# Router scores of a second token block on VectorE, and the last attention chunks two steps later

## The chip, the cores and the metric

The kernel runs on one core of one Trainium2 chip. The metric is device time in microseconds: the median of three runs of the kernel before is 455.16 us (454.08 to 455.33). One execution was profiled: 457.24 us, with a span of 455.1 us from the first instruction to the last.

The engines are TensorE (PE; its weight loads are PEld), VectorE (DVE), ScalarE (ACT), GpSimd (POOL) and SyncE (SP), which here only issues DMAs.

## The reference

Three layers follow each other. Decayed linear attention over 2 batches, 8 heads, 768 positions of 64 dimensions; a feed-forward layer; and a mixture of experts with one expert a token and a skip score:

```
x   = attention(q, k, v, lam)          # (1536, 512) after the heads are joined
h   = x @ w_in                          # 512 -> 2048
g   = where(h > 0, h, exp(min(h, 0)) - 1)
x2  = g @ w_out                         # 2048 -> 512
do  = (x2 @ w_skip) > 0
logits = x2[do] @ w_gate                # 8 experts
e   = argmax(logits); gate = softmax(logits)[e]
out = x2;  out[do] += gate * (relu(x2 @ w1[e]) @ w2[e])
```

The router's scores (8 logits and the skip score) decide comparisons, so they are computed in float32. The large matmuls split each operand into a high part and a residue and multiply in three passes.

## The kernel before

The 1536 tokens are four blocks of 384 (block 0 to 3), each of three chunks of 128 tokens: chunk 0 to 11. Chunks 6 to 8 make block 2, chunks 9 to 11 block 3.

The feed-forward layer runs in 64 units, each one slice of 128 of the 2048 hidden columns for one block. A unit is `ff1_mm` (12 matmuls into a PSUM bank named h, L496), `ff1_act` on ScalarE, the max on VectorE (L516), the high part on ScalarE (L522), the residue on VectorE (`ff1_lo`, L527) and `ff2` (three groups of three matmuls, L543). The units 0 to 31 mix blocks 0 and 1; units 32 to 47 are block 2, 48 to 63 block 3.

From unit 24 on, a loop walks the units. Its step n issues the max and high part of unit n+1, `ff1_mm` of unit n+2, the residue of unit n+1 and `ff2` of unit n. So TensorE alternates one `ff1_mm` and one `ff2`, and VectorE works one unit ahead. There is no scheduler in this stretch: each engine runs in the order in which the code is written. Other work is hung into the steps with five tables, keyed by the step: Y and A after `ff1_mm` (and ahead of the residue), C behind the residue, B behind the second `ff2` group and `ff1_act`, Z behind the third `ff2` group. The helper `put(table, step, function, arguments)` fills them. J is 24, NF 16, N 64, CPB 3, CPS 6.

What is hung in:
- `put_chunks(n, c0)`: attention of three chunks, at steps n, n+2, n+4, n+5. `at_X` issues on TensorE the outputs of the chunk before (L292, 64x64 matmuls) and the key-value products and scores of the next (L364, L330), which share an h bank with `ff1_mm`; then the masks on VectorE (L338). `at_X2` evacuates the chunk before (L427, L431), starts the two state updates (L382, four instructions each) and the query scaling on GpSimd (L345). `at_kdec2` is the key scaling on GpSimd (L350). Before, one state update stands in `at_X2` behind the evacuation and the other in table Z. The sets start at steps 24 and 37.
- `put_routes(n, c0)`: the routing of a block. `route_T` transposes a chunk on TensorE (L583) and copies it to SBUF; `route_logits` is four matmuls by the gate (L598); `route_pick` (L632 to L642), `route_exp`, `route_slot` and `route_send` are small VectorE instructions, with an exponential on ScalarE and an indirect DMA from GpSimd (L700) that scatters the chunk's rows to its experts; `route_rank` is two small matmuls (L655, L658). Block 0 starts at step 37, block 1 at 32, block 2 at 48.
- `route_dots`: for block 0 the scores are not matmuls. VectorE multiplies the chunk by a broadcast gate row and sums in the same instruction (L620, with a second small instruction that reads the accumulator): 9 rows times 3 chunks, 27 products in steps 28 to 37. The gate rows lie in one buffer of the ring `big` (two buffers of 128 x 2048 floats): three rows in turn, the fourth quarter takes the product itself, which nobody reads.
- `conv_piece`: from step 49, the split of one piece of the experts' weights (L138 on ScalarE, L139 on VectorE); `load_pieces` loads two of them into a buffer of `big`.

Of the kernel before, what the change touches and what calls it, by code (L numbers as in the profile page):

```python
# [8 lines left out]
F32 = mybir.dt.float32  # L9
# [4 lines left out]
ALU = mybir.AluOpType  # L14
# [14 lines left out]
LEAD = 21  # L29
TAIL1 = 8  # L30
E = 8
EF = 1024
# [28 lines left out]
def kernel(  # L61
# [49 lines left out]
    places = const.tile([P, P], F32, name="places")  # L111
    rk = const.tile([P, 1], F32, name="rk")
    cnt = const.tile([P, E], F32, name="cnt")
    nx = const.tile([P, E + 1], F32, name="nx")
    nxi = const.tile([P, E + 1], I32, name="nxi")
# [5 lines left out]
    lp = mid.tile([P, 4, P], F32, name="lp")  # L121
    kd = mid.tile([P, H, 1], F32, name="kd")
    state = mid.tile([P, 4, P], F32, name="state")
# [271 lines left out]
    def at_out(c, banks):  # L395
# [7 lines left out]
        for m in range(2):  # L403
            for b, r in ((0, 0), (1, 1), (1, 0), (0, 1)):
                inter(c, r, m, 1 - r, b)

    def at_out2(c):

        nc.tensor.drain()
        for m in range(2):  # L410
            for b, r in ((0, 0), (1, 1), (1, 0), (0, 1)):
                inter(c, r, m, r, b)
# [188 lines left out]

    dots = [(e, c) for e in range(E + 1) for c in range(CPB)]
    dotted, cols = [0], []

    def open_cols():
        t = big(F32).rearrange("p (s d) -> p s d", s=4)
        cols.extend(t[:, i] for i in range(4))
        for e in range(3):
            load_col(e)

    def load_col(e):
        nc.sync.dma_start(out=cols[e % 3], in_=wgt[e:e + 1, :].broadcast_to([P, DM]))

    def route_dots(k):
        for _ in range(k):
            e, c = dots[dotted[0]]
            dotted[0] += 1
            if e == 0:
                lg_t[c] = sm([P, E + 1], F32, "lg", CPB)
            nc.vector.tensor_tensor_reduce(  # L620
                out=cols[3], in0=x2_t[c][:, 0:DM], in1=cols[e % 3], scale=1.0, scalar=0.0,
                op0=ALU.mult, op1=ALU.add, accum_out=lg_t[c][:, e:e + 1])
            if c == CPB - 1 and e + 3 <= E:
                load_col(e + 3)

# [91 lines left out]
    if True:  # L717
# [169 lines left out]

        def at_X2(c, nxt):
            if c is not None:
                at_evac_hi(c)  # L890
                at_evac_lo(c)
                if c == CPS + 1:
                    open_cols()
                elif c == CPS + 2:
                    load_chunk(c + 1)
                elif c + 2 < NCH:
                    load_chunk(c + 2)
            if nxt is not None:
                at_state2(nxt, 0)
                at_qd2(nxt)  # L900
# [4 lines left out]
        def put_routes(n, c0):  # L905
            for i in range(CPB):
                if c0:
                    put(B, n + i, route_T, c0 + i)
# [6 lines left out]
        def put_chunks(n, c0):  # L915
            for c, nxt, m in ((None, c0, n), (c0, c0 + 1, n + 2), (c0 + 1, c0 + 2, n + 4),
# [11 lines left out]
        left = len(dots)  # L928
# [366 lines left out]
```

## Time and profile before

| | |
|---|---|
| median of three runs | 455.16 us (454.08 to 455.33) |
| profiled execution | 457.24 us |
| its span | 455.1 us |
| TensorE busy | 438.2 us, 96% |
| VectorE busy | 314.3 us, 69% |
| ScalarE busy | 241.0 us, 53% |
| GpSimd busy | 78.9 us, 17% |

A step is read from TensorE's timeline: from the first L496 row of one `ff1_mm` to that of the next. Step 24 starts at 143.77 us, step 32 at 185.84, step 37 at 211.22, step 44 at 252.54, step 48 at 269.35. Matmuls are pipelined and their ends are modelled, so a row's length is no measure of a group's cost; the distance from start to start is.

### The profile page before, as it was taken

The page shows a single profiled execution, that of the slowest core. Times are in us where ns is not written, and L with a number is a line of the kernel's source. Part 1 is how long each engine was busy: PE and PEld are TensorE (multiplying, and loading weights), DVE is VectorE, ACT ScalarE, POOL GpSimd, SP SyncE. Part 2 cuts the span into 40 slices and gives each one's busy share as a digit, 9 for nine tenths or more (in the row PEclk, how much of TensorE's full clock was granted, in tenths as well). Part 3 has the DMA queues.
Part 4 walks back from the last instruction along what each step waited for, and adds up shares of the span by engine and source line. Part 5 has one row for each costly group of instructions (what it writes and reads, how often), then busy time and mean ns, then how long its engine had stood idle before and what let it go on. Part 6 is the DMA issues. An engine that isn't in the chain of part 4 may idle for free.

```text
span 455.1 us, 8009 instructions
## 1 busy us (share of the span) xinstructions
PE 438.2 (96%) x3123; PEld 379.5 (83%) x3123; DVE 314.3 (69%) x647; ACT 241.0 (53%) x402; POOL 78.9 (17%) x100
## 2 busy tenths in 40 slices
PE   8889999999999999999999999999999999999993
PEld 7778898879898888988778899889988788888882
DVE  4889999999532448687675225765545789999970
ACT  3456776666444333433232444466642788888840
POOL 4532002201200021014143000220004202222111
PEclk9989999999999999999999999999998999999998
DMA  8999602796001034310320024353446789999300
GB/s 303 401 423 420 238 19 92 232 127 200 0 2 71 5 127 167 125 47 34 108 101 15 0 95 160 118 196 116 149 148 270 256 313 394 371 373 366 144 17 34
DMA packets 27406, 77.07 MB, mean 169 GB/s; under 512 B 4162, under 2 KB 9290, under 8 KB 25312
## 3 DMA queue, kind: packets, MB, share of 16 engines
q1 hardware_dynamic: 25328, 71.35, 44.7%
q0 software_dynamic: 1600, 3.03, 1.8%
q10 hardware_dynamic: 432, 2.10, 1.2%
q8 instruction: 26, 0.43, 0.4%
q14 instruction: 20, 0.16, 0.1%
HBM read 68.18 MB, written 10.51 MB: 173 GB/s over the span
## 4 chain that ended last, share of the span: by engine, by line
PE 66%; DVE 16%; issue 7%; ACT 4%; DMA 4%; POOL 1%; SPq 1%; POOLq 0%; ACTq 0%; DVEq 0%
PE h L496 21%; PE y L543 16%; PE h L1075 8%; PE y L1100 6%; PE aux L543 5%; DVE v L176 3%; DVE v L179 3%; DMA big<-in_wff_dram 2%; ACT v L161 2%; DVE g L527 2%; DVE wa L190 2%; PE aux L598 1%; DVE v L173 1%; PE aux L292 1%; PE aux L1086 1%
## 5 line engine op out<-in xcount | busy, mean ns | idle before, releaser
L496 PE MATMUL h<-xT,wa 128*128 128x384 f32 x480 | 90.8, 340 | 0.6 <-DVE state L382 0.5
L496 PEld LDWEIGHTS h<-xT,wa 128*128 128x128 f32 x480 | 83.9, 188 | 4.3 <-issue 1.1
L543 PE MATMUL y<-wa,g 128*128 128x512 f32 x270 | 70.9, 402 | 1.1 <-DVE g L527 0.9
L522 ACT ACTIVATE g<-e 128x384 fp32r<-128x384 f32 x64 | 33.4, 522 | 48.6 <-DVE e L516 48.6
L543 PEld LDWEIGHTS y<-wa,g 128*128 128x128 f32 x270 | 49.0, 188 | 12.0 <-DVE g L527 1.8
L501 ACT ACTIVATE e<-h 128x384 f32<-128x384 f32 x64 | 31.1, 486 | 51.0 <-PE h L496 50.8
L516 DVE SCALAR_TENSOR_TENSOR e<-e,h 128x384 f32<-128x384 f32 x64 | 35.2, 549 | 32.3 <-ACT e L504 32.3
L496 PE MATMUL h<-xT,wb 128*128 128x384 f32 x288 | 54.7, 339 | 0.9 <-DVE lp L382 0.9
L496 PEld LDWEIGHTS h<-xT,wb 128*128 128x128 f32 x288 | 50.6, 188 | 3.6 <-issue 1.0
L527 DVE TENSOR_TENSOR g<-e,g 128x384 fp32r<-128x384 f32 x64 | 37.6, 588 | 16.0 <-ACT g L522 15.9
L543 PE MATMUL y<-wb,g 128*128 128x512 f32 x162 | 41.0, 397 | 0.2 <-DVE g L527 0.2
L700 POOL DMA_INDIRECT xe<-x,idx x12 | 12.1, 1009 | 141.8 <-DVE s L673 50.3
L1075 PE MATMUL h<-wa,xgT 128*128 128x512 f32 x144 | 36.5, 399 | 0.1
L543 PEld LDWEIGHTS y<-wb,g 128*128 128x128 f32 x162 | 30.0, 188 | 6.5 <-DVE g L527 0.6
L504 ACT ACTIVATE e<-e 128x384 f32<-128x384 f32 x64 | 33.7, 526 | 2.0
L1075 PEld LDWEIGHTS h<-wa,xgT 128*128 128x128 f32 x144 | 26.5, 188 | 6.0 <-ACT xgT L574 0.3
L139 DVE TENSOR_TENSOR wa<-big,wa 128x1024 fp32r<-128x1024 f32 x22 | 26.6, 1234 | 4.5 <-ACT wa L138 4.3
L1100 PE MATMUL y<-wa,ht 128*128 128x512 f32 x96 | 23.9, 400 | 0.0
L139 DVE TENSOR_TENSOR wa<-ahead,wa 128x1024 fp32r<-128x1024 f32 x18 | 21.7, 1248 | 3.0 <-ACT wa L138 2.9
L138 ACT ACTIVATE wa<-big 128x1024 fp32r<-128x1024 f32 x22 | 22.5, 1060 | 1.4 <-DMA big<-in_wex_dram 1.4
L543 PE MATMUL aux<-wa,g 128*128 128x512 f32 x90 | 22.7, 396 | 0.0
L1109 POOL TENSOR_TENSOR o<-o,xg 128x512 f32<-128x512 f32 x7 | 9.0, 1289 | 71.3 <-ACT o L1108 71.3
(225 smaller groups left out, 715.9 us busy)
## 6 DMA issues: line engine op xcount, KB each, us to landing
big<-in_wex_dram SPq DMA_DIRECT2D x17, 1024.0 KB, 4.9
ahead<-in_wex_dram SPq DMA_DIRECT2D x15, 1024.0 KB, 6.2
wb<-in_wff_dram SPq DMA_DIRECT2D x10, 1024.0 KB, 14.1
big<-in_wff_dram SPq DMA_DIRECT2D x5, 1024.0 KB, 11.2
big<-in_kq_dram SPq DMA_DIRECT2D x6, 512.0 KB, 3.3
big<-in_kv_dram SPq DMA_DIRECT2D x6, 512.0 KB, 4.2
out_dram<-x SPq DMA_DIRECT2D x12, 256.0 KB, 2.2
big<-in_wgt_dram SPq DMA_DIRECT2D x9, 256.0 KB, 3.2
```

The costliest lines, as they stand in the source:

```text
L138: nc.scalar.activation(out=w[:, 0, cs], in_=src, func=ACTF.Copy)
L139: nc.vector.tensor_tensor(out=w[:, 1, cs], in0=src, in1=w[:, 0, cs].bitcast(F32), op=ALU.subtract)
L176: nc.vector.scalar_tensor_tensor(out=vi, in0=hi, scalar=-0x80000000, in1=vi, op0=ALU.bitwise_and, op1=ALU.bitwise_or)
L496: nc.tensor.matmul(out=h, lhsT=w[:, wi, k * P:(k + 1) * P], rhs=xT[b][:, xi, k, :], start=(j == 0), stop=(j == 11))
L501: nc.scalar.activation(out=e, in_=h_t[n], func=ACTF.Relu, scale=-1.0)
L504: nc.scalar.activation(out=e_t[n], in_=e_t[n], func=ACTF.Exp, scale=-1.0)
L516: nc.vector.scalar_tensor_tensor(out=e, in0=e, scalar=-1.0, in1=h_t.pop(n), op0=ALU.add, op1=ALU.max)
L522: nc.scalar.activation(out=g[:, 0, :], in_=e, func=ACTF.Copy)
L527: nc.vector.tensor_tensor(out=g[:, 1, :], in0=e_t.pop(n), in1=g[:, 0, :].bitcast(F32), op=ALU.subtract)
L543: nc.tensor.matmul(out=y_t[b, t], lhsT=g[:, gi, t * P:(t + 1) * P], rhs=w[:, wi, 512:1024], start=(f == 0 and i == 0), stop=(f == NF - 1 a ...
L1075: nc.tensor.matmul(out=h, lhsT=xgT_t[e][:, xi, k * P:(k + 1) * P], rhs=w_t[NF + 8 * e + k][:, wi, j * 512:(j + 1) * 512], start=(i == 0), ...
L1100: nc.tensor.matmul(out=y, lhsT=ht[:, hi, k, :], rhs=w_t[NF + 8 * e + 4 + k // 2][:, wi, (k % 2) * 512:(k % 2) * 512 + 512], start=(i == 0) ...
```

## The change

Block 1's scores go the way of block 0's: 27 more products on VectorE, and no `route_T` and `route_logits` for block 1. The number of products in each step from 29 to 49 stands in a tuple. The routing of block 1 starts at step 49 instead of 32, that of block 2 at 52 instead of 48. The second set of chunks starts at step 39 instead of 37. In `at_X2` both state updates come first. The product is written as one byte an element into the storage of `zrow`, a tile of zeros whose last reader is done by then, so the gate rows get all four quarters of their buffer. From step 36 the first half of that buffer takes the keys and queries of chunks 9 to 11, one after the other, and a second buffer their keys and values, in two halves; the gate rows of block 1 use the other two quarters in turn. The load of pieces 2 and 3 of the experts' weights moves from step 48 to 49. Two small tiles share the storage of others.

```diff
+QUOTA = (3, 3, 3, 3, 3, 3, 3, 3, 3, 0, 1, 3, 1, 3, 2, 2, 3, 3, 3, 3, 3)
...
-    rk = const.tile([P, 1], F32, name="rk")
+    rk = cnt[:, 0:1]
...
-    kd = mid.tile([P, H, 1], F32, name="kd")
+    kd = nx[:, 0:H].rearrange("p (h o) -> p h o", o=1)
...
+    junk = zrow.bitcast(mybir.dt.int8)
...
-    dots = [(e, c) for e in range(E + 1) for c in range(CPB)]
+    dots = [(b, e, c) for b in range(2) for e in range(E + 1) for c in range(b * CPB, b * CPB + CPB)]
...
-                out=cols[3], in0=x2_t[c][:, 0:DM], in1=cols[e % 3], scale=1.0, scalar=0.0,
-                op0=ALU.mult, op1=ALU.add, accum_out=lg_t[c][:, e:e + 1])
-            if c == CPB - 1 and e + 3 <= E:
-                load_col(e + 3)
+                out=junk, in0=x2_t[c][:, 0:DM], in1=cols[0][:, slot * DM:(slot + 1) * DM], scale=1.0,
+                scalar=0.0, op0=ALU.mult, op1=ALU.add, accum_out=lg_t[c][:, e:e + 1])
+            if c % CPB == CPB - 1:
+                if b:
+                    load_col(1, e + 2, slot)
+                elif e in (0, 1, 2, 3, 6):
+                    load_col(0, {6: 8}.get(e, e + 4), slot)
+                elif e >= 7:
+                    load_col(1, e - 7, slot)
+
+    def load_late(c):
+
+        if c == CPS + CPB:
+            cols.append(big(F32))
+        kq_t[c] = cols[0][:, 0:1024].rearrange("p (s k i) -> p s k i", s=2, k=4)
+        kv_t[c] = cols[1][:, 1024 * (c % 2):1024 * (c % 2) + 1024].rearrange("p (s d) -> p s d", s=2)
+        dma_kq(c)
+        dma_kv(c)
...
         def at_X2(c, nxt):
+            if nxt is not None:
+                at_state2(nxt, 0)
+                at_state2(nxt, 1)
             if c is not None:
                 at_evac_hi(c)
                 at_evac_lo(c)
...
             if nxt is not None:
-                at_state2(nxt, 0)
                 at_qd2(nxt)
...
-                if c0:
+                if c0 > CPB:
                     put(B, n + i, route_T, c0 + i)
...
-                    put(Z, m, at_state2, nxt, 1)
...
-        put_chunks(2 * NF + 5, CPS + CPB)
...
-        for n in range(J + 4, J + 14):
-            k = min(1 if n == J + 4 else 3, left)
-            left -= k
+        put_chunks(2 * NF + 7, CPS + CPB)
+        for n, k in zip(range(J + 5, 3 * NF + 2), QUOTA):
             if k > 1:
                 put(A, n, route_dots, 1)
-            put(B, n, route_dots, max(1, k - 1))
-        put(Z, J + 13, load_chunk, CPS + CPB + 1)
+            if k:
+                put(B, n, route_dots, max(1, k - 1))
+        put(Z, J + 12, load_late, CPS + CPB)
+        for i in (1, 2):
+            put(B, 2 * NF + 5 + 2 * i, load_late, CPS + CPB + i)
         put_routes(J + 13, 0)
-        put_routes(2 * NF, CPB)
-        put_routes(3 * NF, 2 * CPB)
+        put_routes(3 * NF + 1, CPB)
+        put_routes(3 * NF + 4, 2 * CPB)
...
-                put(B, n, load_pieces, 0)
-                put(B, n, load_pieces, 2)
+                put(B, n, lambda: load_pieces(0, cols[1]))
+                put(B, n + 1, load_pieces, 2)
```

Three places show how the rows of an engine move. The first is TensorE in steps 32 and 33, before (y and h are PSUM banks, x a chunk of block 1, t its transposed copy, wg the gate):

```order
L496 MATMUL h<-xT,wa 128x384 x12
L543 MATMUL y<-wa,g 128x512 x6
L583 MATMUL aux<-ident,x_1910 128x128 x4
L543 MATMUL y<-wa,g 128x512 x3
L496 MATMUL h<-xT,wa 128x384 x12
L598 MATMUL aux<-wg,t_1955 128x9 x4
L543 MATMUL y<-wa,g 128x512 x6
L583 MATMUL aux<-ident,x_1914 128x128 x4
L543 MATMUL y<-wa,g 128x512 x3
```

And the same two steps of the changed kernel (its line numbers are 3 higher here):

```order
L499 MATMUL h<-xT,wa 128x384 x12
L546 MATMUL y<-wa,g 128x512 x9
L499 MATMUL h<-xT,wa 128x384 x12
L546 MATMUL y<-wa,g 128x512 x9
L499 MATMUL h<-xT,wa 128x384 x12
```

The transposes and the logits are gone, and the two matmul groups of a unit follow each other directly.

The second place is VectorE in step 39, from the masks (t) to the next max; before, this is the entry with the outputs of chunk 9 and the scores of chunk 10 (xT the evacuation, lp and state the state updates):

```order
L338 TENSOR_TENSOR t_2436<-h,mask 128x256
L632 TENSOR_REDUCE mx<-lg 128x1
L634 SCALAR_TENSOR_TENSOR dact<-lg,desc 128x8
L637 SCALAR_TENSOR_TENSOR eqd_92<-lg,mx,dact 128x8
L640 TENSOR_REDUCE m_2444<-eqd_92 128x1
L642 TENSOR_SCALAR pick<-eqd_92,m_2444 128x8
L527 TENSOR_TENSOR g<-e,g 128x384
L431 TENSOR_TENSOR xT<-aux,xT 128x4x64 x2
L382 SCALAR_TENSOR_TENSOR lp<-state,lp,h 128x64 x4
```

In the changed kernel step 39 is the entry with the scores of chunk 9 and no outputs (L628 is the product with the one-byte output in zrow):

```order
L339 TENSOR_TENSOR t_2221<-h,mask 128x256
L654 TENSOR_REDUCE mx<-lg 128x1
L656 SCALAR_TENSOR_TENSOR dact<-lg,desc 128x8
L659 SCALAR_TENSOR_TENSOR eqd_92<-lg,mx,dact 128x8
L662 TENSOR_REDUCE m_2229<-eqd_92 128x1
L664 TENSOR_SCALAR pick<-eqd_92,m_2229 128x8
L530 TENSOR_TENSOR g<-e,g 128x384
L383 SCALAR_TENSOR_TENSOR state<-lp,h 128x64 x4
L383 SCALAR_TENSOR_TENSOR state<-state,lp,aux 128x64 x4
L628 ISA zrow,lg<-x_1905,big 128x512
L628 ISA lg 128x1
```

The evacuation is no longer between the residue and the first state; both states stand together, and a product follows them.

The third place is VectorE in the entry with the outputs of chunk 9 and the scores of chunk 10, step 41 of the changed kernel; before it was the stretch of step 39 above:

```order
L339 TENSOR_TENSOR t_2434<-h,mask 128x256
L530 TENSOR_TENSOR g<-e,g 128x384
L383 SCALAR_TENSOR_TENSOR lp<-state,lp,h 128x64 x4
L383 SCALAR_TENSOR_TENSOR state<-lp,aux 128x64 x4
L434 TENSOR_TENSOR xT<-aux,xT 128x4x64 x2
L628 ISA zrow,lg<-x_1909,big 128x512
L628 ISA lg 128x1
```

No pick stands between the masks and the residue there, and the evacuation comes behind both states.

## Rows read from the trace of the kernel before

**Rows 1.** The page: busy time of each engine, share of the span, instructions.
```profile
PE 438.2 (96%) x3123; PEld 379.5 (83%) x3123; DVE 314.3 (69%) x647; ACT 241.0 (53%) x402; POOL 78.9 (17%) x100
```

**Rows 2.** Busy time by stretch: PE, PEld, DVE, ACT, POOL, clock, DMA.
```profile
252.54:269.35 16.81, 16.81 (x86) 15.17 (x85) 4.34 (x8) 6.44 (x13) 0.00 (x0) 1.00 0.00 0
185.84:211.22 25.38, 25.38 (x149) 22.64 (x147) 20.43 (x78) 9.03 (x20) 3.65 (x5) 1.00 0.21 74
211.22:256.76 45.54, 42.96 (x544) 36.54 (x542) 26.25 (x103) 14.89 (x34) 12.18 (x20) 1.00 0.17 58
```

**Rows 3.** TensorE's timeline, step 33: start, length, line, tiles, count.
```profile
192.55 0.95 PE L598 MATMUL aux<-wg,t 128*128 128x9 f32 x8
```

**Rows 4.** TensorE's timeline, first matmuls of steps 37 to 42, idle before.
```profile
211.22 2.28 PE L496 MATMUL h<-xT,wa 128*128 128x384 f32 x12
...
218.47 2.32 PE L496 MATMUL h<-xT,wa 128*128 128x384 f32 x12 [0.49 <-DVE state L382]
...
222.80 2.34 PE L496 MATMUL h<-xT,wa 128*128 128x384 f32 x12
...
231.15 2.35 PE L496 MATMUL h<-xT,wb 128*128 128x384 f32 x12 [0.91 <-DVE lp L382]
...
235.51 2.34 PE L496 MATMUL h<-xT,wb 128*128 128x384 f32 x12
...
242.48 2.32 PE L496 MATMUL h<-xT,wb 128*128 128x384 f32 x12
```

**Rows 5.** VectorE's timeline, steps 39 and 40: state, first and last of a pick.
```profile
230.26 0.84 DVE L382 SCALAR_TENSOR_TENSOR lp<-state,lp,h 128x64 f32<-128x64 f32 x4
...
234.06 0.15 DVE L632 TENSOR_REDUCE mx<-lg 128x1 f32<-128x8 f32 x1
...
234.78 0.23 DVE L642 TENSOR_SCALAR pick<-eqd,m 128x8 bf16<-128x8 f32 x1
```

**Rows 6.** Products of line 620 (min/median/max ns); timelines of VectorE and GpSimd.
```profile
L620 DVE CUSTOM_DVE_ANT_0 big<-x,big x27: 681/685/1699, 171.3 to 218.2; 128x512 f32<-128x512 f32 x27
...
210.16 1.70 DVE L620 CUSTOM_DVE_ANT_0 big<-x,big 128x512 f32<-128x512 f32 x1
...
210.25 1.06 POOL L350 TENSOR_TENSOR big<-big,mask 128x512 f32<-128x512 f32 x1
...
240.41 1.79 POOL L345 TENSOR_TENSOR mask<-big,lp 128x256 f32<-128x256 f32 x2 [2.91 <-PE aux L292]
```

**Rows 7.** VectorE's timeline: the maxes of steps 30 and 52, a split.
```profile
177.79 0.55 DVE L516 SCALAR_TENSOR_TENSOR e<-e,h 128x384 f32<-128x384 f32 x1
...
180.81 0.56 DVE L516 SCALAR_TENSOR_TENSOR e<-e,h 128x384 f32<-128x384 f32 x1
...
291.62 0.55 DVE L516 SCALAR_TENSOR_TENSOR e<-e,h 128x384 f32<-128x384 f32 x1
...
293.72 1.23 DVE L139 TENSOR_TENSOR wa<-big,wa 128x1024 fp32r<-128x1024 f32 x1 [0.39 <-ACT wa L138]
...
295.43 0.55 DVE L516 SCALAR_TENSOR_TENSOR e<-e,h 128x384 f32<-128x384 f32 x1
```

**Rows 8.** Timelines of TensorE and VectorE: step 24, closing halves of 26 and 27.
```profile
143.77 2.28 PE L496 MATMUL h<-xT,wb 128*128 128x384 f32 x12
...
147.96 0.55 DVE L527 TENSOR_TENSOR g<-e,g 128x384 fp32r<-128x384 f32 x1
...
158.08 2.37 PE L543 MATMUL aux<-wb,g 128*128 128x512 f32 x9
...
160.38 2.32 PE L496 MATMUL h<-xT,wb 128*128 128x384 f32 x12
...
162.53 2.26 PE L543 MATMUL aux<-wb,g 128*128 128x512 f32 x9
...
164.63 2.28 PE L496 MATMUL h<-xT,wb 128*128 128x384 f32 x12
```

**Rows 9.** The page's DMA issues: KB each, median us from issue to landing.
```profile
big<-in_kv_dram SPq DMA_DIRECT2D x6, 512.0 KB, 4.2
```

More of the change, by code (lines that the diff above doesn't have):

```diff
@@ L599, in route_logits, with load_col @@
                              start=(k == 0), stop=(k == 3))
-    dots = [(e, c) for e in range(E + 1) for c in range(CPB)]
-    dotted, cols = [0], []
+    dots = [(b, e, c) for b in range(2) for e in range(E + 1) for c in range(b * CPB, b * CPB + CPB)]
+    dotted, cols, col_of = [0], [], {}
     def open_cols():
[L606 to L612, printed above, removed]
+        t = big(F32)
+        cols.append(t)
+        for e in range(4):
+            load_col(0, e, e)
+    def load_col(b, e, slot):
+        if b < 2 and e <= E:
+            col_of[b, e] = slot
+            nc.sync.dma_start(out=cols[0][:, slot * DM:(slot + 1) * DM],
+                              in_=wgt[e:e + 1, :].broadcast_to([P, DM]))
     def route_dots(k):
         for _ in range(k):
-            e, c = dots[dotted[0]]
+            b, e, c = dots[dotted[0]]
             dotted[0] += 1
             if e == 0:
-                lg_t[c] = sm([P, E + 1], F32, "lg", CPB)
+                lg_t[c] = sm([P, E + 1], F32, "lg", 4)
+            slot = col_of[b, e]
             nc.vector.tensor_tensor_reduce(
-                out=cols[3], in0=x2_t[c][:, 0:DM], in1=cols[e % 3], scale=1.0, scalar=0.0,
-                op0=ALU.mult, op1=ALU.add, accum_out=lg_t[c][:, e:e + 1])
-            if c == CPB - 1 and e + 3 <= E:
-                load_col(e + 3)
+                out=junk, in0=x2_t[c][:, 0:DM], in1=cols[0][:, slot * DM:(slot + 1) * DM], scale=1.0,
[14 more added lines that the diff above has]
+        dma_kv(c)
     def route_pick(c):
@@ L893, in at_X2 @@
                     open_cols()
-                elif c == CPS + 2:
-                    load_chunk(c + 1)
-                elif c + 2 < NCH:
+                elif c == CPS:
                     load_chunk(c + 2)
             if nxt is not None:
-                at_state2(nxt, 0)
                 at_qd2(nxt)
@@ L922, in put_chunks @@
                         put(B, m - 1, at_kdec2, nxt)
-                    put(Z, m, at_state2, nxt, 1)
         at_kdec2(CPS)
         put_chunks(J, CPS)
-        put_chunks(2 * NF + 5, CPS + CPB)
-        left = len(dots)
-        for n in range(J + 4, J + 14):
-            k = min(1 if n == J + 4 else 3, left)
-            left -= k
+        put_chunks(2 * NF + 7, CPS + CPB)
+        for n, k in zip(range(J + 5, 3 * NF + 2), QUOTA):
             if k > 1:
                 put(A, n, route_dots, 1)
-            put(B, n, route_dots, max(1, k - 1))
-        put(Z, J + 13, load_chunk, CPS + CPB + 1)
+            if k:
[3 more added lines that the diff above has]
+            put(B, 2 * NF + 5 + 2 * i, load_late, CPS + CPB + i)
         put_routes(J + 13, 0)
-        put_routes(2 * NF, CPB)
-        put_routes(3 * NF, 2 * CPB)
+        put_routes(3 * NF + 1, CPB)
+        put_routes(3 * NF + 4, 2 * CPB)
         for n in range(3 * NF, N):
```

## The prediction

> **What bounds the kernel now.** I read the page first. TensorE is busy 96% of the span of 455.1 us; the profiled execution took 457.24 us, 2.1 us of it outside the span [rows 1]. With an engine that full the question is narrower: in which steps does it need longer than in a plain step, and is the extra its own work or a wait? So I went to the busy times by stretch, cut at the first matmul (L496) of a step. Four plain steps (44 to 47) take 16.81 us, 4.20 us each. The five steps 32 to 36, which route block 1, take 25.38 us with TensorE busy in all of it; the eight steps 37 to 44, with the last block's chunks, take 45.54 us with TensorE busy in 42.96 [rows 2]. The first is extra work, the second work and waits. TensorE's timeline shows the extra work, transposes (L583) and logits (L598) between the feed-forward matmuls; one group of logits stands in the rows [rows 3]. For the waits I read the same timeline by step starts [rows 4]: step 37 lasts 7.25 us (211.22 to 218.47), 38 4.33, 39 8.35, 40 4.36, 41 6.97; 42 has the 5.88 that these and two plain steps leave of 45.54. The rows that close 37 and 39 name VectorE's state update (L382) as what TensorE waited for. On VectorE it stood last in step 39, behind masks, a pick, the residue of g and the evacuation, and ended at 231.10 [rows 5], just before TensorE went on at 231.15.
>
> **Block 1's scores move to VectorE.** TensorE loses three groups of four transposes and three of logits; VectorE loses two copies of the transposed block (ScalarE one) and gains 27 products with their accumulator reads. With nothing in their place steps 32 to 36 are plain, 5 x 4.20 = 21.0 against 25.38: 4.38 us saved. Block 1's three rank matmuls do not go, they move to steps 50 to 52. Step 40, whose only extra is a rank, took 4.36 against 4.20, so 3 x 0.16 = 0.48 is given back: 3.90 net.
>
> The cover for the products is VectorE's spare time. A product takes 685 ns at the median [rows 6]. In step 30, plain with three products, VectorE goes from one max (L516) to the next in 3.02 us, 177.79 to 180.81 [rows 7], and the step has 4.20: 1.18 us spare. Steps 30 to 37 and 45 to 48 have that load. Step 49 adds a weight split of 1.23 us, 4.25 in all, just over a step. Steps 51 to 55 hold a split and a whole routing: step 52 before, with all of that but the pick and the exponent's inputs, went from max to max in 3.81 us (291.62 to 295.43) [rows 7]; a pick adds 0.95 (234.06 to 235.01) [rows 5], so some 4.8 us in 51 and 52, while 53 to 55 are made longer by block 2's own transposes. The residue of g is due only a step later, so VectorE has about a step of lead. I put 0.2 us, between 0 (all inside the lead) and 1.5 (1.2 in 51 and 52, the rest later).
>
> The product's output now takes one byte an element. No row shows that; the nearest is the same product with four-byte output, 681 to 1699 ns [rows 6]. Nothing suggests less than 681, since both four-byte inputs still stream in; 1699 bounds it above. I take the median, 685, and keep the upper end as a rival.
>
> **The last block's chunks two steps later.** Before, block 0's routing (steps 38 to 41) met chunks at 37, 39, 41 and 42; now they stand at 39, 41, 43 and 44, so the light entry, which evacuates nothing, meets the picks.
> - 37 plain 4.20; 38 keeps its rank, 4.33.
> - 39, first scores and states with a pick between masks and residue. In step 24, the same entry with no pick, the residue ended 4.74 us after the start (143.77 to 148.51) [rows 8]; a pick of 0.95 and a state of 0.84 more give 6.5. Step 37, the same entry with a product there, took 7.25; the pick is 0.26 longer: 7.5. I take 7.0.
> - 40: VectorE comes late. Before, the way from the state's end (231.10) to the pick of step 40 (234.06) took 2.96 us [rows 5]; now two products lie on it too, and the pick is 0.95: the rank may start 2.96 + 1.38 + 0.95 = 5.3 us into the step, or 4.5 if the 0.8 that GpSimd's scaling held VectorE up there does not recur. TensorE gets there after 4.2. I take 5.1 for the step: a wait that takes an old one's place, with the whole next step queued behind it.
> - 41: the state now ahead of the evacuation. Before, its closing feed-forward half took 2.30 us, as in steps 26 and 28 (158.08 to 160.38), against 2.10 in a plain step (162.53 to 164.63) [rows 8]. That 0.2 goes: 6.77.
> - 42 plain, 4.20. 43 has a product where the evacuation stood, about as long, so it keeps 6.97. 44 is the old last one, 5.88.
> Sum 44.45 against 45.54: 1.09 saved, between -0.9 (39 at 8.35, 40 at 5.6) and +2.3 (6.5 and 4.36).
>
> **States first in the first set.** Steps 26 and 28 lose the same 0.2 each: 0.40 saved. The evacuation comes up to 1.7 us (two states) later; its banks' next user is two steps off.
>
> **The loads.** All late chunks share one key and query buffer, so chunk 11's load waits on SP for GpSimd's query scaling in step 41, and the next gate row queues behind it. That scaling ended at 242.20 (240.41 and 1.79) [rows 6], as step 42 began. The half with keys and values lands 4.2 us after issue [rows 9], about when step 43 begins; the key scaling takes 1.06, and TensorE asks for it after the feed-forward half and the outputs, some 2.8 us into that step. I cost it at nothing, with about a microsecond of cover; if that is gone, chunk 11's states are late by as much. Pieces 2 and 3 of the expert weights load a step later, with a step left before their split. The small tiles that now share storage (L112, L122) are used at the two ends of the program: nothing.
>
> **Sum.** 3.90 + 1.09 + 0.40 - 0.20 = 5.19 us: 457.24 becomes 452.05 in a profiled execution. That one lies 2.08 above the median of the runs shown, 455.16 (454.08 to 455.33), so I forecast 450.0 us there.
>
> **Rivals.** (a) *Products meet GpSimd.* One product took 1699 ns, from 210.16, while GpSimd's scaling ran from 210.25 for 1.06 us [rows 6]: VectorE was held for the scaling's length. If that happens wherever TensorE waits for VectorE (the state of 39, the rank of 40, the state of 43), 0.8 us each beyond the sum, 2.4 us go: 452.4. For it: steps 39 to 43 now hold nine products. Against: most scalings start while VectorE waits for scores. The Trainium skill (SBUF — State Buffer, "SBUF: two separate sides") has the two engines share a port pair as an exclusive lock, a VectorE operation with two SBUF inputs against a GpSimd one that reads SBUF. By that rule every such meeting costs up to the whole scaling, which is this rival's sum; the trace agrees, 1699 being 685 and 1014 more.
> (b) *Slower: the byte output is dear.* Spare is 1.18 us in a three-product step, 0.39 a product. At twice 685 a step would need 5.07, 0.87 over, in 13 steps (30 to 37, 45 to 49): 11.3 us lost against 5.2 gained, 461.3. It decides from about 1.2 us a product. For: nothing here writes bytes at that length. Against: the inputs alone account for the row.
> (c) *The time comes back later.* If the expert stage, after step 60, ran at the pace of its weights' loads, an earlier start would be worth nothing: 455.2. For: the loads start from the same buffers as before, and two pieces even later. Against: the stretch by stretch view has TensorE busy throughout steps 32 to 36 and plain steps alike, and the whole span at 96%, so no later stage hides a wait of that size.
>
> **How the numbers follow.** Forecast 0.68, own range 447.8 to 451.8: down if the waits of 39 and 40 vanish, up if both come at their upper ends and the late routing costs 0.5 more. Rival (a) 0.17, 451.8 to 453.6, faster still. (c) 0.09, (b) 0.06. The range, 447.8 to 453.5, leaves out (b), (c) and little else. A measurement of this kernel tells about 0.3%, 1.4 us, from no change: faster 0.85, same 0.09, slower 0.06.
>
> **What would show it.** Right: steps 32 to 36 at 4.2 us, with no L583 or L598 there; products near 0.69 us; 39 and 40 near 7.0 and 5.1, the latter closed by a rank that waited for VectorE's pick; 41 at 6.8. Wrong: products over 0.8 us; TensorE waiting for VectorE in steps 45 to 55; a key scaling in 42 or 43 waiting for a DMA; an expert stage longer by what the steps before it saved.

## The result and the profile after

The changed kernel takes 448.29 us (median of four runs, 447.2 to 449.8) against 455.25 us (454.08 to 456.58) for the kernel before (median of four): a ratio of 0.9845, 95% interval 0.9805 to 0.9884. The forecast was 450.0 us, range 447.8 to 453.5. The profiled execution took 447.47 us, its span is 445.7 us (455.1 before). The ratios here and below leave out two executions at a much lower granted clock, one of `better` (605.47 us) and one of the kernel before beside `b_states`, `b_chunks39` and `before_again` (711.98 us); the medians do not.

The page's line on the engines, which answers to [rows 1]: TensorE loses 36 instructions and 12 us of busy time, VectorE gains 52 instructions and 15 us.

```profile
PE 426.2 (96%) x3087; PEld 371.2 (83%) x3087; DVE 329.1 (74%) x699; ACT 240.0 (54%) x401; POOL 80.2 (18%) x100
```

The busy times by stretch (start and end, length, PE, PEld, DVE, ACT, POOL, granted clock, DMA share, GB/s) of steps 32 to 36, 37 to 44, 48 to 56 and 57 to 60, of the last routing (from its first L1039), and of the expert stage from its first L1096 to the start of its last group of matmuls (L1121):

```profile
183.75:204.58 20.83, 20.83 (x107) 18.90 (x105) 15.97 (x43) 8.41 (x17) 0.00 (x0) 1.00 0.22 75
204.58:249.43 44.85, 42.18 (x543) 36.39 (x542) 32.06 (x120) 14.27 (x33) 13.14 (x18) 1.00 0.32 107
261.93:305.16 43.23, 42.91 (x239) 37.77 (x237) 32.72 (x120) 23.28 (x44) 6.29 (x10) 1.00 0.45 157
305.16:321.83 16.67, 16.67 (x86) 15.12 (x85) 10.38 (x18) 10.07 (x17) 2.60 (x5) 1.00 0.46 156
334.05:338.30 4.25, 4.17 (x41) 3.95 (x40) 3.23 (x24) 0.85 (x4) 0.00 (x0) 1.00 1.03 421
...
338.30:429.43 91.13, 90.84 (x441) 74.67 (x442) 79.25 (x119) 72.50 (x97) 21.76 (x18) 1.00 0.80 296
```

The first two answer to [rows 2]: 25.38 became 20.83, 45.54 became 44.85. The same view of the kernel before, for the other four:

```profile
269.35:311.58 42.23, 42.23 (x233) 37.88 (x231) 25.54 (x71) 23.28 (x42) 4.96 (x9) 1.00 0.45 154
311.58:328.38 16.80, 16.80 (x86) 15.16 (x84) 9.35 (x12) 10.03 (x17) 0.00 (x0) 1.00 0.41 142
340.70:346.54 5.84, 5.75 (x42) 5.44 (x41) 3.40 (x23) 0.86 (x4) 0.00 (x0) 0.71 1.03 402
...
346.53:438.67 92.14, 91.89 (x442) 74.80 (x442) 79.36 (x117) 72.52 (x97) 21.68 (x18) 1.00 0.76 287
```

The 9.4 us between the spans lie in three places. The start, up to step 24, is 1.6 shorter (142.19 against 143.77). Steps 24 to 60 are 4.97 shorter (179.64 against 184.61), close to the 5.19 forecast for them. What follows step 60 is 2.82 shorter (123.92 against 126.74): 1.59 in the last routing, where the granted clock before was 0.71 (a mean of its two levels, 1.2 and 2.4 GHz) and now is 1.00, and 1.01 in the expert stage, at clock 1.00 in both. The prediction had no term for the start, the last routing or the expert stage.

What TensorE waits for in steps 37 to 44 now (tile and line, releaser, us in total, times, longest):

```profile
PE aux L680 <- DVE pick L664: 1.1, 1, 1.1
PE h L499 <- DVE state L383: 1.1, 2, 0.7
PE aux L293 <- issue: 0.3, 2, 0.2
```

The steps 37 to 44 last 4.17, 4.23, 6.51, 5.59, 6.96, 4.19, 7.30 and 5.90 us. The two rows that close 39 and 40, which answer to [rows 4], name VectorE's state and its pick:

```profile
219.49 0.41 PE L499 MATMUL h<-xT,wb 128*128 128x384 f32 x1 [0.75 <-DVE state L383]
...
225.05 0.17 PE L680 MATMUL aux<-pick,ustrict 128*128 128x8 bf16 x1 [1.14 <-DVE pick L664]
```

The product, which answers to the first of [rows 6], takes with its one-byte output what it took with four bytes, and here none of the 54 was held up:

```profile
L628 DVE CUSTOM_DVE_ANT_0 zrow<-x,big x54: 672/685/693, 170.7 to 272.8; 128x512 int8<-128x512 f32 x54
```

### The profile page after: what moved, and what is told of

Its sections match the earlier page's. It is cut to its first block, busy times and chain, and to the rows that moved or that the text cites. A ratio compares the mean times of both kernels' runs of the same rounds, so it can differ in the third digit from the quotient of the medians.

```text
span 445.7 us, 8024 instructions
## 1 busy us (share of the span) xinstructions
PE 426.2 (96%) x3087; PEld 371.2 (83%) x3087; DVE 329.1 (74%) x699; ACT 240.0 (54%) x401; POOL 80.2 (18%) x100
## 4 chain that ended last, share of the span: by engine, by line
PE 66%; DVE 16%; issue 6%; ACT 4%; DMA 4%; POOL 1%; SPq 1%; POOLq 0%; ACTq 0%; DVEq 0%
PE h L499 21%; PE y L546 15%; PE h L1096 8%; PE y L1121 6%; PE aux L546 5%; DVE v L177 3%; DVE v L180 2%; DMA xe<-blank 2%; ACT v L162 2%; DMA big<-in_wex_dram 1%; DVE g L530 1%; DVE wa L191 1%; PE aux L293 1%; DVE wa L140 1%; DVE v L174 1%
## 5 line engine op out<-in xcount | busy, mean ns | idle before, releaser
L546 PE MATMUL y<-wa,g 128*128 128x512 f32 x270 | 69.1, 397 | 1.3 <-DVE g L530 0.9
L628 DVE CUSTOM_DVE_ANT_0 zrow<-x,big 128x512 int8<-128x512 f32 x54 | 37.0, 686 | 0.6
L1096 PE MATMUL h<-wa,xgT 128*128 128x512 f32 x144 | 36.0, 397 | 0.1
L1096 PEld LDWEIGHTS h<-wa,xgT 128*128 128x128 f32 x144 | 26.5, 188 | 5.7 <-ACT xgT L577 0.3
L1121 PE MATMUL y<-wa,ht 128*128 128x512 f32 x96 | 23.7, 397 | 0.0
```

The costliest lines, as they stand in the source:

```text
L546: nc.tensor.matmul(out=y_t[b, t], lhsT=g[:, gi, t * P:(t + 1) * P], rhs=w[:, wi, 512:1024], start=(f == 0 and i == 0), stop=(f == NF - 1 a ...
L628: nc.vector.tensor_tensor_reduce(out=junk, in0=x2_t[c][:, 0:DM], in1=cols[0][:, slot * DM:(slot + 1) * DM], scale=1.0, scalar=0.0, op0=ALU ...
L1096: nc.tensor.matmul(out=h, lhsT=xgT_t[e][:, xi, k * P:(k + 1) * P], rhs=w_t[NF + 8 * e + k][:, wi, j * 512:(j + 1) * 512], start=(i == 0), ...
L1121: nc.tensor.matmul(out=y, lhsT=ht[:, hi, k, :], rhs=w_t[NF + 8 * e + 4 + k // 2][:, wi, (k % 2) * 512:(k % 2) * 512 + 512], start=(i == 0) ...
```

## The experiments

Ratios are against the kernel before, on the chip of that run, with their 95% intervals. `again`, `chunks37`, `states_late` and `scores_only` ran first, then `no_ks10`, `picks_early`, `piece_early` and `better`, then `b_states`, `b_chunks39` and `before_again`, and `b_layout` last; those of a group share a chip.

**`again`: the changed kernel, a second time.** No edit.

> The changed kernel once more, for its time and a second trace. My theory: only steps 24 to 60 were shortened by the change, by about 5 us (184.61 to 179.64 in the first two traces); the 4.4 us that the first trace after gained besides, 1.6 before step 24 and 2.8 after step 60, differ from execution to execution. It expects steps 24 to 60 within 0.3 us of 179.64, the other two parts to differ by a microsecond or more from the first trace, and a ratio near 0.988. Rival: the expert stage is shorter by the change itself, because its weights' loads or VectorE's backlog stand better; it expects 123.9 us from step 61 to the end again, and a ratio near 0.984.

Measured: 448.53 us, 0.9868 (0.9842 to 0.9895), span 446.1. Steps 24 to 60 take 179.96 us, the stretch behind them 124.05; step by step the trace agrees with the first within 0.1 us, but for step 50 (4.35 instead of 4.70) and step 41, which takes 7.82 us instead of 6.96. The parts ahead of step 24 and behind step 60 come out as in the first trace (142.11 and 124.05), which the rival had and not the theory. In step 41 TensorE stands for 0.37 us, with nothing shown that it waits for, and the groups on both sides run slower:

```profile
228.24 0.22 PE L365 MATMUL h<-big 64*64 64x64 f32 x1
228.83 0.24 PE L365 MATMUL h<-big 64*64 64x64 f32 x1 [0.37 <-issue]
```

All six other traces that have this entry in step 41 and products on VectorE show 7.80 to 8.11 us, so 6.96 is the exception: comparisons in steps 37 to 44 are best made with `again` (45.64 us). What holds TensorE there stays open.

**`chunks37`: the late chunks back at step 37,** with their loads in the shared buffers two steps earlier too, so that scores and states stay as changed.

```diff
-        put_chunks(2 * NF + 7, CPS + CPB)
+        put_chunks(2 * NF + 5, CPS + CPB)
...
-        put(Z, J + 12, load_late, CPS + CPB)
+        put(Z, J + 10, load_late, CPS + CPB)
...
-            put(B, 2 * NF + 5 + 2 * i, load_late, CPS + CPB + i)
+            put(B, 2 * NF + 3 + 2 * i, load_late, CPS + CPB + i)
```

> The changed kernel with the last chunks at steps 37, 39, 41, 42 instead of 39, 41, 43, 44; states first. My theory: the collision of chunk outputs, a pick and a rank in step 39 comes back, but with the state ahead of the evacuation it costs less than the 8.35 us of before, about 7.6, and the rank then waits for the evacuation: steps 37 to 44 together 45.0 to 46.0 us against 44.85 in the changed kernel, 0.2 to 1.2 us slower than it. Rival: the two steps' shift is worth nothing, since the waits only move (39 fell by 1.84, 40 and 43 rose by 1.23 and 0.33): 44.6 to 44.9 us.

Measured: 453.4 us, 0.9967 (0.9948 to 0.9986). Steps 37 to 44 take 50.29 us, 5.4 more than in the first trace of the changed kernel and 4.65 more than in `again`; no theory had that. Step 39 alone takes 12.51. GpSimd's key scaling of chunk 10 waited for its DMA and TensorE for that scaling (the waits of step 39, then GpSimd's timeline):

```profile
PE h L365 <- POOL big L351: 2.9, 1, 2.9
```

```profile
219.42 1.06 POOL L351 TENSOR_TENSOR big<-big,mask 128x512 f32<-128x512 f32 x1 [17.56 <-DMA big<-in_kv_dram]
```

SP's queue shows why the transfer was late: the load of chunk 10 (L232, L235) stands behind a gate row's load (L618), which could only be issued at 212.14, when block 0's last product had been read out (212.11).

```profile
212.14 0.33 SPq L618 DMA_DIRECT2D big<-in_wgt_dram  x1
212.64 0.33 SPq L232 DMA_DIRECT2D big<-in_kq_dram  x1
213.02 0.42 SPq L235 DMA_DIRECT2D big<-in_kv_dram  x1
```

And the wait costs more than its 2.9 us, since the granted clock fell during it to 0.50, the lower level of 1.2 GHz, and was still there 5.8 us after TensorE went on at 220.53 (the same step by stretch):

```profile
214.44:219.40 4.96, 3.19 (x63) 2.81 (x62) 0.59 (x4) 1.54 (x3) 0.00 (x0) 1.00 0.68 228
219.50:226.30 6.80, 5.59 (x87) 4.71 (x88) 3.61 (x17) 0.66 (x2) 2.83 (x3) 0.50 0.01 2
226.40:226.95 0.55, 0.55 (x6) 0.26 (x4) 0.55 (x2) 0.00 (x0) 0.00 (x0) 1.00 0.68 238
```

So in the company of the shared buffers the shift is needed to get chunk 10 loaded in time.

**`states_late`: the states back in their old places,** all else as changed.

```diff
-            if nxt is not None:
-                at_state2(nxt, 0)
-                at_state2(nxt, 1)
...
+                at_state2(nxt, 0)
...
+                    put(Z, m, at_state2, nxt, 1)
```

> The changed kernel with the states where they stood before: the first behind the evacuation, the second at the end of the step. My theory: steps 26 and 28 go back to about 6.9 us from 6.81 and 6.78, that is by 0.1 to 0.2 each, 41 from 6.96 to 7.1 or more, 39 unchanged at 6.5 (it evacuates nothing): 0.3 to 0.7 us slower than the changed kernel. Rival: the order of states and evacuation is worth nothing, since VectorE's next max comes at the same time either way: all four within 0.05 us.

Measured: 451.6 us, 0.9925 (0.9897 to 0.9952). Steps 26 and 28 take 6.92 and 6.89 again (6.81 and 6.78 with states first), 40 takes 5.84 and 43 takes 8.23 (7.30), since the state is behind the evacuation there:

```profile
PE h L499 <- DVE state L383: 1.1, 1, 1.1
```

Steps 24 to 60 take 182.16 us, 2.5 and 2.2 more than in the two traces of the changed kernel, more than any theory had. Of the first, 1.0 is step 41's gap; of the second, 0.4 lies behind step 44, in step 50, and 1.8 up to step 44.

**`scores_only`: the last two edits together,** chunks at 37 and states in their old places.

> The changed kernel with the last chunks at step 37 as before and with the states in their old places; block 1's scores on VectorE, its later routing, the gate rows and the byte output stay. My theory (the parts add up): steps 32 to 36 at 4.17 us each, so 4.5 us of the gain less some 1.0 us in steps 48 to 56, and steps 37 to 44 no shorter than the 45.5 us of before, since picks and products again meet the chunks: net 3 to 4 us under the kernel before, 452 us or a ratio near 0.992. Rival (the three parts hang together: products in the chunk steps make the old positions dearer than before): steps 37 to 44 at 47 us or more, and a ratio of 0.995 or above.

Measured: 453.04 us, 0.9967 (0.9942 to 0.9991). Steps 32 to 36 take 20.73, but 37 to 44 take 48.94, with the same wait for chunk 10's scaling in step 39 (1.9 us, step 39 at 10.83). So the rival had it right: most of what the scores give is lost four steps on, though by the late load and not by picks and products alone.

**`b_chunks39`: the shift alone, in the kernel before,** where each chunk has a buffer of its own.

```diff
-        put_chunks(2 * NF + 5, CPS + CPB)
+        put_chunks(2 * NF + 7, CPS + CPB)
```

> The kernel before with one edit: the last block's chunks start at step 39 instead of 37; each chunk keeps its own buffer, loaded as before, and block 1's scores stay on TensorE. Theory (the shift by itself is worth little, its 4 to 5 us in the changed kernel are the room that it gives the load of chunk 10 in the shared buffer): steps 37 to 44 stay at 45.5 within 1 us, the whole within 1 us of before, and no step among 39 to 44 has TensorE waiting for GpSimd or a DMA. Rival (the prediction: the light entry meeting the picks saves 1.1 us together with the states): 37 to 44 fall to 44.4 to 44.8. Second rival (the shift is worth as much here as in the changed kernel): they fall to 42 or less.

Measured: 452.77 us, 0.9958 (0.993 to 0.9986). Steps 37 to 44 take 43.35 us, 2.19 less than before: between the theories, and twice the prediction's 1.09. Busy times of the stretch, and what TensorE waits for there:

```profile
209.66:253.01 43.35, 42.20 (x543) 36.15 (x542) 26.14 (x101) 15.25 (x34) 13.62 (x20) 1.00 0.19 61
```

```profile
PE h L496 <- DVE gsum L692: 0.7, 1, 0.7
PE aux L292 <- issue: 0.3, 2, 0.2
```

Step 40 takes 4.34 us and its rank waits for nothing; no product stands ahead of the pick there. So light entries that meet the picks are worth 2.2 us. In the changed kernel, with products in these steps, most or all of it is lost again: step 40 takes 1.25 more, 43 takes 0.39 more, and 41, in `again`, 0.85.

**`b_states`: states first alone, in the kernel before.**

```diff
+            if nxt is not None:
+                at_state2(nxt, 0)
+                at_state2(nxt, 1)
...
-                at_state2(nxt, 0)
...
-                    put(Z, m, at_state2, nxt, 1)
```

> The kernel before with one edit: both state updates come first in at_X2, ahead of the evacuation. Theory (the states are what TensorE waits for, and they pay only where VectorE is late): steps 26 and 28 fall by 0.1 each as in the changed kernel (6.92 to 6.81 and 6.78), 39 falls from 8.35 to 7.2 to 7.7 because the second state no longer stands last behind evacuation, 41 by 0.1 to 0.2; the whole by 0.9 to 1.5 us, to about 454.1. Rival (the prediction's sizes: 0.2 in each of 26, 28 and 41, nothing elsewhere): 39 stays at 8.2 or more, the whole falls by 0.6. Second rival (what the states gave in the changed kernel, 2.2 us from 24 to 60, is theirs in any company): steps 24 to 60 fall by 2 us or more.

Measured: 454.59 us, 0.998 (0.9961 to 1.0). Steps 26 and 28 fall to 6.79 as expected, but 39 grows from 8.35 to 9.08, which no theory had, and 37 to 44 take 46.15 (45.54 before). What TensorE waits for in step 39:

```profile
PE aux L655 <- DVE state L382: 1.4, 1, 1.4
...
PE h L364 <- POOL big L350: 0.3, 1, 0.3
```

Before, TensorE went on in step 39 after the evacuation, 0.74 us, and one state [rows 5], 0.84 us:

```profile
229.59 0.74 DVE L431 TENSOR_TENSOR xT<-aux,xT 128x256 fp32r<-128x256 f32 x2
```

Now the rank waits for both states, 0.84 each. The second state took the evacuation's place in the wait, so nothing is gained; and the masks came 0.55 us later (4.73 instead of 4.18 us into the step), 0.30 of it by the wait for GpSimd's key scaling in the second row. In step 43 of the changed kernel there is one state only, and there the evacuation's time does go.

**`no_ks10`: GpSimd's key scaling of chunk 10 left out.**

```diff
-                        put(B, m - 1, at_kdec2, nxt)
+                        if nxt != CPS + CPB + 1:
+                            put(B, m - 1, at_kdec2, nxt)
```

> The changed kernel without GpSimd's scaling of chunk 10's keys (that part of the computation is left out; chunk 10's states are then built from unscaled keys). In the changed kernel step 40 took 5.59 us, with the rank waiting 1.14 us for the pick, one small instruction of which took 1.50 us instead of 0.23 while this scaling ran on GpSimd. Theory (GpSimd holds VectorE there): that instruction falls to about 0.23 us, the rank's wait to 0.2 or less, step 40 to 4.3 to 4.6 us, the whole by 0.9 to 1.2 us to about 447.3 us. Rival (the pick is late because two products and the states lie ahead of it, as the prediction's sum of 5.1 has it): step 40 stays at 5.1 or more and the whole within 0.5 us of the changed kernel's 448.4.

Measured: step 40 takes 4.31 us instead of 5.59, as the theory had it, and the rank's wait is gone; 447.74 us, 0.9845 (0.9811 to 0.988). The interval holds the changed kernel's ratios, so the whole does not tell; the trace does. Step 41 took 7.83 here, as in `again`, and against `again` steps 37 to 44 fall from 45.64 to 44.42. In the changed kernel a pick's small instruction on VectorE, and GpSimd beside it:

```profile
222.85 0.15 DVE L656 SCALAR_TENSOR_TENSOR dact<-lg,desc 128x8 f32<-128x8 f32 x1
223.04 1.50 DVE L659 SCALAR_TENSOR_TENSOR eqd<-lg,mx,dact 128x8 f32<-128x8 f32 x1
224.57 0.16 DVE L662 TENSOR_REDUCE m<-eqd 128x1 f32<-128x9 f32 x1
```

```profile
223.45 1.05 POOL L351 TENSOR_TENSOR big<-big,mask 128x512 f32<-128x512 f32 x1
```

Without the scaling:

```profile
222.79 0.23 DVE L659 SCALAR_TENSOR_TENSOR eqd<-lg,mx,dact 128x8 f32<-128x8 f32 x1
```

VectorE's instruction ends at 224.54, as the scaling ends (224.50). The Trainium skill (SBUF — State Buffer, "SBUF: two separate sides") has VectorE and GpSimd hold a common port pair for a whole instruction, the loser blocked; for this instruction the trace agrees, 1.50 against 0.23. By the recorded starts VectorE's instruction was first, by 0.41 us, and alone it would have ended before the scaling; GpSimd's spans are rough in these profiles, so who was first is not shown.

**`picks_early`: all three picks of block 0 in step 38,** where VectorE has neither masks nor states.

```diff
-                put(A, n + 1 + i, route_pick, c0 + i)
+                put(A, n + 1 + (i if c0 else 0), route_pick, c0 + i)
```

> The changed kernel with the three picks of block 0 all in step 38, where VectorE has neither masks nor states, instead of one each in 38, 39 and 40. Theory (the picks are what makes VectorE late in 39 and 40): 39 falls from 6.51 to about 5.8 us, 40 from 5.59 to 4.3 to 4.4, step 38 stays at 4.2 to 4.5, the whole falls by 1.5 to 2.0 us to about 446.6. Rival (VectorE's backlog is only moved one step ahead): 38 grows by 0.7 or more, 39 and 40 fall by as much, and the whole stays within 0.7 us of 448.4.

Measured: 446.82 us, 0.9815 (0.9788 to 0.9842). Step 38 stays at 4.23, 39 takes 5.66, 40 takes 4.30; 37 to 44 take 43.77 us even with 8.04 in step 41. The theory holds by the trace (the intervals of the whole overlap with the changed kernel's); the backlog does not move one step ahead. GpSimd's scaling of chunk 10 now meets a product instead of a pick, and the product is held:

```profile
222.67 1.82 DVE L628 CUSTOM_DVE_ANT_0 zrow<-x,big 128x512 int8<-128x512 f32 x1
```

```profile
222.88 1.06 POOL L351 TENSOR_TENSOR big<-big,mask 128x512 f32<-128x512 f32 x1
```

Nothing on TensorE waits for that product, so its 1.1 us cost nothing.

**`piece_early`: the load of the first two weight pieces in step 46 instead of 48.**

```diff
-                put(B, n, lambda: load_pieces(0, cols[1]))
+                put(B, n - 2, lambda: load_pieces(0, cols[1]))
```

> The changed kernel with the load of the first two pieces of the experts' weights issued two steps earlier, in step 46 instead of 48. In the changed kernel ScalarE's first split waited 3.47 us for it in step 49, and the rank of step 50 waited 0.32 us for a pick that stood behind VectorE's half of that split. Theory (the load is the wait): ScalarE's wait goes to under 0.5 us, step 50 falls from 4.70 to about 4.3, the whole by 0.3 to 0.5 us, to about 448.0. Rival (VectorE's load of product, split and routing sets steps 50 to 52 anyway): 48 to 56 stay at 43.2 within 0.2 us in all.

Measured: ScalarE's split starts at 267.64 without a wait and step 50 takes 4.22 us instead of 4.70 (4.35 in `again`); 48 to 56 take 42.43 (43.23 and 42.90). In the changed kernel this stood there:

```profile
269.88 1.06 ACT L139 ACTIVATE wa<-big 128x1024 fp32r<-128x1024 f32 x1 [3.47 <-DMA big<-in_wex_dram]
```

Step 50 alone would not show this: in `no_ks10` and `picks_early`, with the load in step 48, it takes 4.22 too. But the load landed earlier there, 5.95 and 5.73 us after its issue instead of 6.55, and in all seven traces with the load in step 48 the step grows with that time, from 4.22 (5.73) over 4.35 (6.21) to 4.77 (6.58). The whole, 448.73 us, 0.9863 (0.983 to 0.9897), is not told apart from the changed kernel: 0.5 us is too little for these intervals.

**`better`: the last two edits, and all products of steps 40 and 43 behind the residue.**

```diff
-            if k > 1:
+            a = 1 if k > 1 and n not in (2 * NF + 8, 2 * NF + 11) else 0
+            if a:
...
-                put(B, n, route_dots, max(1, k - 1))
+                put(B, n, route_dots, k - a)
```

> The changed kernel with three things: block 0's picks all in step 38, the first weight pieces loaded in step 46, and all products of steps 40 and 43 in the last table of the step, behind the residue. Theory (each of the three waits is VectorE being late, and they are apart from each other): 39 about 5.8, 40 4.3 to 4.4, 43 about 6.9 instead of 7.3, 50 about 4.3; together 2.0 to 2.7 us less, 445.6 to 446.5. Rival (a wait taken away comes back at the next instruction that needs VectorE): the sum of steps 37 to 56 falls by less than 1 us, and the whole stays at 447.5 or more.

Measured: 446.39 us, 0.9804 (0.9775 to 0.9834), the lowest of all; `piece_early`, on the same chip, takes 2.3 us more, and the two intervals just touch. Steps 37 to 44 take 43.18 us, 48 to 56 take 42.49; 39, 40, 43 and 50 take 5.66, 4.31, 6.76 and 4.23. In 37 to 44 no wait for VectorE is left, only step 41's gap, longer here:

```profile
PE h L365 <- issue: 0.8, 1, 0.8
PE aux L293 <- issue: 0.2, 1, 0.2
```

Steps 37 to 56 fall by 2.4 us against the first trace of the changed kernel, so the waits did not come back elsewhere.

**`before_again`: the kernel before, a second trace.** No edit.

> The kernel before once more, for a second trace of it. Of the 9.4 us between the two spans, 1.6 lie ahead of step 24 (143.77 against 142.19 us) and 2.8 behind step 60 (126.74 against 123.92), where the change leaves nearly all instructions as they were. Theory (these two vary from execution to execution): step 24 starts at 142 to 143.3 us and the stretch behind step 60 takes 124 to 126 us, apart from the first trace by 0.7 us or more in one of them. Rival (the change shortens them): both come within 0.4 us of the first trace. Steps 24 to 60 take 184.6 within 0.5 us by either.

Measured: 455.14 us, span 453.4. Step 24 starts at 142.16 us, so the start's 1.6 us vary from execution to execution and are no work of the change. Steps 24 to 60 take 184.48. Behind them it takes 126.77, as before: that half of the theory fell for this kernel. But the last routing alone splits all traces in two: with the mean granted clock at 0.7 there, the time behind step 60 is 126.7 (before, twice), and with the clock at 1.00 it is 125.1 (`b_states`, `b_chunks39`), with the same code. Of the kernels built on the changed one, those at 0.7 take 125.55 to 125.85 (`chunks37`, `states_late`, `no_ks10`, `picks_early`), those at 1.00 take 123.92 to 124.54. So a lower clock costs 1.6 us there; what decides it is open. The 1.0 us that is left between 125.1 and 124.0 is another cause.

**`b_layout`: the kernel before with the storage edits alone.** The engines get the same instructions in the same order.

```diff
-    rk = const.tile([P, 1], F32, name="rk")
+    rk = cnt[:, 0:1]
...
-    kd = mid.tile([P, H, 1], F32, name="kd")
+    kd = nx[:, 0:H].rearrange("p (h o) -> p h o", o=1)
...
-                lg_t[c] = sm([P, E + 1], F32, "lg", CPB)
+                lg_t[c] = sm([P, E + 1], F32, "lg", 4)
```

> The kernel before with only the storage edits of the change: two small tiles share the storage of others, and the logits tile has four buffers instead of three, so that the tiles behind them lie at other addresses; the instructions and their order are those of before. In steps 57 to 60, where every engine does the same in all traces, a step took 4.20 us in all four traces of kernels built on before and 4.15 to 4.17 in all nine built on the changed one. Theory (where the tiles lie sets this pace): steps 57 to 60 take 16.6 to 16.7 us instead of 16.8, the expert stage from its first L1075 about 1.0 us less, the whole 1.2 to 2.0 us less, to about 453.7. Rival (something else of the change sets it, such as what VectorE or the DMA queues do beside): 16.80 us and the whole within 0.6 us of before's 455.3, but for the start and the last routing, which vary from execution to execution.

Measured: 452.26 us, 0.9939 (0.9919 to 0.9959). Steps 57 to 60 take 16.67 us, the expert stage 1.0 less, both as in the changed kernel (the last routing here had the lower clock):

```profile
309.25:325.92 16.67, 16.67 (x86) 15.12 (x84) 9.35 (x12) 9.97 (x17) 0.00 (x0) 1.00 0.42 141
338.14:343.95 5.81, 5.72 (x41) 5.41 (x41) 3.38 (x23) 0.85 (x4) 0.00 (x0) 0.71 1.03 398
344.00:435.10 91.10, 90.82 (x442) 74.65 (x442) 79.24 (x117) 72.47 (x97) 21.73 (x18) 1.00 0.77 290
```

Steps 24 to 60 take 183.81, 0.80 less than before. The theory holds: this saves 1.8 us in the trace and, timed, 0.6% (0.4 to 0.8), about 2.8 us (1.9 to 3.7). The third edit, a fourth buffer for the logits, belongs to the change too, though the prediction named the two tiles alone. As the two kernels are built, each engine's instructions stand in the same order, the feed-forward weights (wa, wb) lie 32 bytes lower in each partition, `big`, ahead, xgT and ht lie 32 bytes higher, and xT and g stay where they were. Which of the three edits does it, and by what property of the addresses, was not tried.

## Why the prediction was right, point by point

| step of the prediction | forecast | measured | of it storage (`b_layout`) |
|---|---|---|---|
| scores off TensorE, steps 32 to 36 | -4.38 | -4.55 | -0.05 |
| three ranks and late routing, 48 to 56 | +0.68 | +1.00; `again` +0.67 | -0.24 |
| last chunks later, 37 to 44 | -1.09 | -0.69; `again` +0.10 | -0.05 |
| states first, 24 to 29 | -0.40 | -0.44 | -0.17 |
| storage, all of 24 to 60 | 0 | | -0.80 |
| storage, expert stage | 0 | -1.01 | -1.04 |
| start, last routing | 0 | -1.58, -1.59; clock and execution | |

The main term was right, in size and cause: five plain steps with three products each, and 685 ns a product. Rival (b) is out by the product's row, rival (c) because nothing came back behind step 60.

**The step that failed is the one costed at nothing: "the small tiles that now share storage".** It was argued from who uses the tiles, and they are used at the two ends only. But their removal moves what lies behind them, and TensorE's pace in plain steps went from 4.20 to 4.17 us. With the expert stage that is 1.8 us in the trace, and about 2.8 timed (`b_layout`, which also has the fourth logits buffer). A row-by-row sum of changed work cannot see a change in the pace of unchanged work.

**That the number came out is in part luck, by misses of opposite sign.** Without the 0.80 of storage the changed work saved 4.17 us in steps 24 to 60, and 3.85 in `again`: 1.0 to 1.3 less than the sum of 5.19. The storage, with no term, gave more than that back, 1.8 us. So the two make 6.0 of the 7.0 us between the medians, and the measured 448.3 lies 1.7 under the forecast of 450.0. The range does not follow from the sum at its ends either: with 39 and 40 at 6.5 and 4.36 the sum comes to about 448.7 (448.5 with nothing for the late routing), not 447.8; with 8.35 and 5.6 the chunks lose 0.8, not 0.9, and with 0.5 more for the late routing the upper end is 452.3, not 451.8. So the measured time lies just under the lowest that the terms of the sum allow.

**The late chunks were mis-sized, in parts that cancel.** The shift itself is worth 2.2 us (`b_chunks39`), not 1.1: 39 at 6.5 instead of 7.0, and 40 with no wait for the pick. The products then cost it back. Step 40 took 5.59 (forecast 5.1), and the wait was the rank's for VectorE's pick, as named; but it was not made by the two products. One instruction of the pick took 1.27 us longer beside GpSimd's scaling, and without the scaling, with both products in place, the step takes 4.31 (`no_ks10`). The 5.1 stood near the 5.3 that kept the old hold of 0.8; the hold came back, and longer. So rival (a)'s mechanism is real at the rank of 40, where it holds a small instruction; a product is held the same way once the picks are gone (`picks_early`), but there TensorE does not wait for it. Step 43 took 7.30 (forecast 6.97), with a wait of 0.34 for the state behind this residue:

```profile
241.62 1.09 DVE L530 TENSOR_TENSOR g<-e,g 128x384 fp32r<-128x384 f32 x1
```

```profile
241.09 2.22 POOL L346 TENSOR_TENSOR mask<-big,lp 128x256 f32<-128x256 f32 x2 [3.32 <-PE aux L293]
```

It took 1.09 us instead of 0.55 beside GpSimd's query scaling. In `better`, with the product behind it, it takes 0.55 and the wait is gone; whether the product ahead or the hold made the wait is not separated. Step 41 was forecast at 6.77, and mostly takes 7.8, by the open gap.

**States first** was priced by 26, 28 and 41 alone. In the changed kernel it is worth 1.8 us from 24 to 44 (`states_late` against `again`), in the kernel before nothing (`b_states`). The prediction added the edits up; the runs show that they lean on each other. Without the shift the load of chunk 10 into the shared buffer comes late and step 39 takes 12.51 us (`chunks37`), 4.16 more than before. The sum, with the loads at nothing, is right only for the place in which they are: there chunk 11's key scaling did wait 0.34 us for its load, a sign named against, but it was done at 237.77 and TensorE asked for it at 239.20, so the cover held:

```profile
236.50 1.27 POOL L351 TENSOR_TENSOR big<-big,mask 128x512 f32<-128x512 f32 x1 [0.34 <-DMA big<-in_kv_dram]
```

**Late routing** held: TensorE did wait for VectorE in step 50, 0.32 us, which I had named a sign against; its source was the time at which the load of piece 0 landed (`piece_early` and the seven traces beside it), not VectorE's count of instructions.

## What to carry to other kernels

Sum the changed work, but run the storage edits of a change alone too: here moving tiles in SBUF by 32 bytes was worth 1.8 us in the trace, about half of what the main edit gave net of the late routing. Where edits share a queue, a buffer or an engine, price them together; the same reordering was worth 1.8 us in one company and nothing in another. When work moves to an engine with spare time, look for the few instructions that another engine waits for, put the moved work behind them, and give them a step where GpSimd is not on the same data path.

## What the runs showed of the hardware

- TensorE's pace changed with storage edits alone (`b_layout`). In steps 57 to 60 a 512-column matmul of the second layer starts 233.3 ns after the one before it (mean of 32 pairs in the timeline) in all four traces with the old addresses, and 230.2 or 229.1 in the ten with new ones, at granted clock 1.00 in each. Which operand's address it is stays open.
- A VectorE instruction of 128x8 takes 1.50 us instead of 0.23 beside GpSimd's scaling. In the changed kernel none of the 54 products took over 0.69, though the one at 241.02 ran beside GpSimd's query scaling of 241.09 to 243.31; with the pick out of the way a product met the key scaling and took 1.82 (`picks_early`) and 2.09 us (`better`).
- In a wait of 2.9 us TensorE's granted clock fell to half, and it was 0.50 from 219.5 to 226.3 us, mostly with TensorE at work (`chunks37`). In the last routing the same code runs at a mean granted clock of 0.7 or of 1.00, 1.6 us apart.
